# Backward-pass side jobs in another order, and one piece of a zero fill copied inside HBM

## The chip, the cores and the metric

The kernel runs on one core of one Trainium2 chip. Its time is device time in microseconds (us), the median of three runs. A profile of one execution stands beside it: its span is the time from the first to the last instruction that the profiler saw. Besides the compute engines TensorE (PE), VectorE (DVE), ScalarE (ACT) and GpSimd (POOL), the core has 16 DMA engines that carry every transfer. Two engines issue transfers here: SP puts them on the hardware queue (q1 in the profile), POOL on the software queue (q0). Both queues run on the same 16 DMA engines.

## The reference

One token passes a layer of grouped-query attention over the last W = 4096 rows of a key and a value cache, and a gated linear feed-forward layer; wanted are the output and the gradients of eight inputs, everything in bfloat16:

```python
k = jnp.repeat(k_cache[:, :, Sk - W:, :], rep, axis=1)      # Sk = 32768, W = 4096, 8 kv heads, Dh = 256
v = jnp.repeat(v_cache[:, :, Sk - W:, :], rep, axis=1)
scores = jnp.einsum("bhqd,bhkd->bhqk", q, k) * (Dh ** -0.5)
o = jnp.einsum("bhqk,bhkd->bhqd", _softmax(scores), v)
h = x + (o reshaped) @ wo
h2 = h + ((hn @ w_gate) * (hn @ w_up)) @ w_down             # hn = layernorm(h)
_out, _vjp = jax.vjp(_f, A_x, A_k_cache, A_v_cache, A_wq, A_wo, B_w_gate, B_w_up, B_w_down)
return (h2, *grads)
```

The gradients of the two caches have the caches' full shape (8 heads x 32768 rows x 256), and only the last 4096 rows of each head can be other than zero. So 2 x 8 regions of 28672 rows are zeros that the kernel has to write: 234.88 MB. The window parts of these gradients are 33.6 MB, the windows that are read some 34 MB, and the gradients of the weights (outer products of two vectors) are small beside them.

## The kernel before

**The fill.** A tile `zeros` of 128 x 8192 bfloat16 (16 KB in a partition) is cleared by DVE (line 54). SP then issues 16 transfers, one for each head `g` and each cache gradient (`out_2` for the keys, `out_3` for the values; lines 55 to 58). Each writes one region of 14,336 KB: seven pieces of 16 KB for each partition, all read from `zeros`. SP does nothing else. The hardware queue holds a bit more than two of them, and SP stands in the issue of the next until there is room.

**Everything else** goes through POOL's queue (`IO`): the small vectors `x_bf` and `go_bf` (lines 88, 90), the weights, the K and V windows of 2 MB each (line 75), and all other outputs.

**Forward** (up to line 399): for each of eight heads, scores, softmax and moments, then the feed-forward layer; eight slots of `S` hold windows and weights in turn.

**Backward** (lines 400 to 445): the gradients of the feed-forward layer's gates, then of `h`, then `doT`, and at line 453 `dq`. Behind it stand eight stages, one for each kv head `g` (lines 546 to 595). A stage transposes the V window on PE (line 554), forms `dp` (line 559), builds rows for an outer product (line 572), and in 16 steps of line 588 makes the gradients of 4096 key rows and 4096 value rows in PSUM, which ACT and DVE copy in turn into two of four staging slots of `S` (helper `evac`, lines 210 and 212). Two transfers of 2 MB store them (line 593). A stage may use a staging slot only when the stores of two stages before have landed.

**Side jobs.** After its stores each stage runs jobs from the table `side` (lines 521 to 531): `outer` (lines 472 to 477) writes one part of a weight gradient: DVE scales rows into one of two staging buffers of `Mt` (line 476) and POOL stores it (line 477), so a third call waits until the first one's store has landed. `ffn_out` (lines 490 to 501) loads `w_down` again and makes the output `h2`. `dxn_part` (lines 507 to 511) loads a part of `wq` again into `Rt` (4 of 7 blocks, then 3), and DVE multiplies it with `dq` and sums (line 510); `dx_out` then finishes the gradient of `x`. The second part goes into the same place in `Rt` as the first and must wait for it; the first must wait for `ffn_out`, which keeps `w_down` there.

The program's order is the order of the text only roughly: a scheduler places the instructions of each engine, and each engine then runs its own list strictly in order. So an instruction of a side job that waits for a transfer holds up what stands behind it on its engine.

Of the kernel before, what the change touches and what calls it, by code (L numbers as in the profile page):

```python
# [7 lines left out]
bf16 = mybir.dt.bfloat16  # L8
# [5 lines left out]
D = 448  # L14
# [4 lines left out]
W = 4096  # L19
# [3 lines left out]
Sk = 32768  # L23
# [5 lines left out]
HQ = H * Dh // 2  # L29
HF = F // 2  # L30
ZW = 8192
NZ = (Sk - W) * Dh // (128 * ZW)
# [8 lines left out]
def kernel(  # L41
# [4 lines left out]
    FILL = nc.sync  # L46
    IO = nc.gpsimd

    const = ctx.enter_context(tc.tile_pool(name="const", bufs=1))
    small = ctx.enter_context(tc.tile_pool(name="small", bufs=2))  # L50
    ps = ctx.enter_context(tc.tile_pool(name="ps", bufs=1, space=bass.MemoryType.PSUM))

    zeros = const.tile([128, ZW], bf16)
    V_.memset(zeros[:], 0.0)
    for g in range(G):
        for o in (out_2, out_3):
            reg = o[0, g, 0:Sk - W, :].rearrange("s d -> (s d)").rearrange("(p n f) -> p n f", p=128, f=ZW)
            FILL.dma_start(out=reg, in_=zeros[:].unsqueeze(1).to_broadcast([128, NZ, ZW]))


    S = const.tile([128, NS, SLOT], bf16)
# [22 lines left out]
        return w.rearrange("a b -> (a b)").rearrange("(p x) -> p x", p=128)  # L84


    x_bf = const.tile([1, D], bf16, tag="rowa", name="x_bf")
    IO.dma_start(out=x_bf[:], in_=A_x.rearrange("a b d -> (a b) d"))
    go_bf = const.tile([1, D], bf16, tag="rowb", name="go_bf")
    IO.dma_start(out=go_bf[:], in_=grad_out.rearrange("a b d -> (a b) d"))  # L90
    wq_sb = S[:, 1:3, :].rearrange("p a b -> p (a b)")[:, 0:NI * HQ]
    IO.dma_start(out=wq_sb, in_=flat_rows(A_wq))
    load_K(0)
# [126 lines left out]
    rstd1, xh1, xf1, xx1 = layernorm(xX[:], "ln1")  # L220
# [121 lines left out]
    bc2 = [S[:, 7, NI * HF:NI * HF + F].rearrange("p (i c) -> p i c", i=2), Rt[:, NI * HF:NI * HF + F].rearrange("p (i c) -> p i c", i=2)]  # L342
# [43 lines left out]
    rstd2, xh2, xf2, xx2 = layernorm(hX[:], "ln2")  # L386
# [44 lines left out]
    dh_bc = const.tile([128, D], bf16)  # L431
# [30 lines left out]
    dq_bc = late[:, 0:2 * HQ].rearrange("p (i c) -> p i c", i=2)  # L462
# [41 lines left out]
    wq2 = Rt[:, 0:4 * HQ].rearrange("p (i c) -> p i c", c=HQ)  # L504
    wq_d = flat_rows(A_wq).rearrange("p (i c) -> p i c", i=NI)

    def dxn_part(i0, i1):
        IO.dma_start(out=wq2[:, 0:i1 - i0, :], in_=wq_d[:, i0:i1, :])
        for i in range(i0, i1):
            V_.tensor_tensor_reduce(out=wq2[:, i - i0, :], in0=wq2[:, i - i0, :], in1=dq_bc[:, i % 2, :], scale=1.0, scalar=0.0,  # L510
                                    op0=ALU.mult, op1=ALU.add, accum_out=Pq[:, i:i + 1])

    def dx_out():
# [4 lines left out]
        V_.tensor_copy(out=dx[:], in_=t[:])  # L518
        IO.dma_start(out=out_1.rearrange("a b d -> (a b) d"), in_=dx[:])

    side = {
        0: [lambda: outer(o6, 0, 4, lambda i: bc2[0][:, i % 2, :], xf2, HF), lambda: outer(o6, 4, 7, lambda i: bc2[0][:, i % 2, :], xf2, HF),
            lambda: outer(o7, 0, 4, lambda i: bc2[1][:, i % 2, :], xf2, HF), lambda: outer(o7, 4, 7, lambda i: bc2[1][:, i % 2, :], xf2, HF)],
        1: [ffn_out] + [lambda b=b: outer(o5, b, b + 8, lambda n: dh_bc[:], oT_f, D) for b in (0, 8)],
        2: [lambda b=b: outer(o5, b, b + 8, lambda n: dh_bc[:], oT_f, D) for b in (16, 24)],
        3: [lambda b=b: outer(o8, b, b + 7, lambda n: dh2_bc[:], hh, D) for b in (0, 7)],
        4: [lambda: dxn_part(0, 4)],
        5: [lambda: dxn_part(4, 7), dx_out],
        6: [lambda i=i: outer(o4, i, min(i + 2, 7), lambda n: dq_bc[:, n % 2, :], xf1, HQ) for i in (0, 2)],
        7: [lambda i=i: outer(o4, i, min(i + 2, 7), lambda n: dq_bc[:, n % 2, :], xf1, HQ) for i in (4, 6)],  # L530
    }


    STG = [5, 6, 7, 0]
# [91 lines left out]
```

## Time and profile before

| what | value |
|---|---|
| time, median of 3 runs | 818.56 us (818.16 to 818.86) |
| the profiled execution: its time, its span | 818.39 us, 816.6 us |
| busy: PE, DVE, ACT, POOL | 497.6, 376.8, 164.9, 41.7 us |
| moved by DMA | 338.66 MB, mean 415 GB/s |
| of it hardware queue (the fill) | 234.88 MB, 68.2% of the DMA engines' span |
| of it software queue | 103.00 MB, 30.2% |
| HBM read, written | 57.28 MB, 280.59 MB |

The shares of the two queues are the time that their packets took, as a part of 16 engines' span. A share of DMA near 1 in a stretch means that all 16 DMA engines moved packets all the time in it (packets that overlap slightly can bring it to 1.01). The compute engines are all far from full, so what one of them waits for matters only where a transfer starts late by it and a DMA engine stands idle for that.

### The profile page before, as it was taken

How to read it: one execution, taken by the hardware profiler on the slowest of the kernel's cores; microseconds unless marked ns; L12 is line 12 of the kernel's file. 1: busy time of each engine (PE TensorE's matmuls, PEld its weight loads, DVE VectorE, ACT ScalarE, POOL GpSimd, SP SyncE). 2: the span in 40 equal slices, each digit the busy share in tenths (PEclk: the TensorE clock that was granted, in tenths of full speed). 3: DMA queues.
4: the chain of work that ended last, by engine and by line, in shares of the span. 5: the costliest groups of instructions: out<-in, count | busy, mean ns of one | idle time of the engine just before them, and what ended most of it. 6: DMA issues, size and time to landing. Idle time of an engine off the chain costs nothing.

```text
span 816.6 us, 12117 instructions
## 1 busy us (share of the span) xinstructions
PE 497.6 (61%) x4947; PEld 300.9 (37%) x4991; DVE 376.8 (46%) x1149; ACT 164.9 (20%) x261; POOL 41.7 (5%) x77
## 2 busy tenths in 40 slices
PE   3558869999574946062993468799378940001770
PEld 3545646666343523031981332345124410001110
DVE  4127847667461643028732354565255440404550
ACT  0220201221101000000011233355244420000440
POOL 4000000000000001000000000010010000000000
PEclk9959888999695969565555556555555555555555
DMA  8999999999999999999999999999999999999985
GB/s 322 431 424 429 427 429 426 429 427 426 432 423 426 424 420 418 427 429 432 423 430 427 417 413 426 428 402 429 419 404 426 423 428 400 424 415 432 431 355 237
DMA packets 24632, 338.66 MB, mean 415 GB/s; under 512 B 1312, under 2 KB 1376, under 8 KB 4736
## 3 DMA queue, kind: packets, MB, share of 16 engines
q1 hardware_dynamic: 14592, 234.88, 68.2%
q0 software_dynamic: 9984, 103.00, 30.2%
q8 instruction: 39, 0.64, 0.3%
q14 instruction: 17, 0.14, 0.0%
HBM read 57.28 MB, written 280.59 MB: 414 GB/s over the span
## 4 chain that ended last, share of the span: by engine, by line
issue 50%; DMA 22%; PE 14%; another core or an unknown queue 4%; DVE 4%; POOL 2%; ACT 1%; POOLq 0%; DVEq 0%; ACTq 0%
DMA out_dram<-Mt 9%; DMA out_dram<-S 5%; DMA S<-in_A_wo_dram 4%; PE dq_ps L453 3%; PE d_ps L588 3%; PE tr L554 2%; DMA S<-in_A_v_cache_dram 2%; DMA S<-in_A_wq_dram 2%; PE MT L322 2%; DVE Rt L423 1%; DVE Rt L510 1%; POOL S L75 1%; PE dh_ps L159 1%; DVE S L212 1%
## 5 line engine op out<-in xcount | busy, mean ns | idle before, releaser
L322 PE MATMUL MT<-Rt,S 128*128 128x512 bf16 x468 | 146.7, 391 | 22.5 <-DMA S<-in_A_v_cache_dram 19.8
L588 PE MATMUL d_ps<-R,Mt 32*128 32x512 bf16 x256 | 121.1, 605 | 58.6 <-DVE S L212 57.9
L318 DVE TENSOR_SCALAR Rt<-S,pf 128x256 bf16<-128x256 bf16 x512 | 118.0, 282 | 31.6 <-PE acc L329 16.5
L212 DVE CAST S<-d_ps 128x512 bf16<-128x512 f32 x128 | 87.1, 689 | 63.4 <-ACT S L210 55.6
L210 ACT CAST S<-d_ps 128x512 bf16<-128x512 f32 x128 | 74.9, 586 | 127.7 <-PE d_ps L588 127.7
L266 PE MATMUL tr<-ident_bf,S 128*128 128x128 bf16 x512 | 51.5, 264 | 43.4 <-DMA S<-in_A_k_cache_dram 40.1
L325 PEld LDWEIGHTS <-S 128*128 128x128 bf16 x512 | 50.1, 99 | 62.9 <-issue 7.2
L554 PE MATMUL tr<-ident_bf,S 128*128 128x128 bf16 x512 | 67.6, 304 | 0.7 <-ACT Mt L210 0.7
L588 PEld LDWEIGHTS <-Mt 32*128 32x128 bf16 x256 | 22.8, 113 | 112.8 <-issue 110.8
L329 PE MATMUL acc<-ones_bf,Rt 128*128 128x1 bf16 x1024 | 62.0, 164 | 0.0
L554 PEld LDWEIGHTS <-S 128*128 128x128 bf16 x512 | 48.4, 136 | 24.4 <-issue 24.4
L266 PEld LDWEIGHTS <-S 128*128 128x128 bf16 x512 | 40.5, 120 | 41.9 <-DMA S<-in_A_k_cache_dram 40.6
L325 PE MATMUL acc<-pT_all,S 128*128 128x2 bf16 x512 | 49.3, 166 | 2.6 <-issue 0.9
L165 PE MATMUL t<-st,ones_f 128*128 128x2 f32 x4 | 1.2, 364 | 79.6 <-DVE st L196 79.6
L210 ACT COPY Rt<-tr 128x1024 bf16<-128x1024 bf16 x32 | 32.4, 1012 | 85.1 <-PE tr L266 84.6
L210 ACT COPY Mt<-tr 128x1024 bf16<-128x1024 bf16 x32 | 32.4, 1014 | 60.8 <-PE tr L554 34.3
L329 PEld LDWEIGHTS <-Rt 128*128 128x128 bf16 x1024 | 44.5, 96 | 0.0
L212 DVE COPY Rt<-tr 128x1024 bf16<-128x1024 bf16 x32 | 22.1, 689 | 47.5 <-PE tr L266 46.2
L322 PEld LDWEIGHTS <-S 128*128 128x128 bf16 x512 | 32.2, 97 | 22.3 <-DMA S<-in_A_v_cache_dram 20.0
L331 ACT COPY Mt<-MT 128x512 f32<-128x512 f32 x8 | 4.7, 586 | 165.1 <-remote 73.8
L510 DVE CUSTOM_DVE_ANT_0 Rt<-Rt,Mt 128x2048 bf16<-128x2048 bf16 x7 | 15.6, 2289 | 48.3 <-DMA Rt<-in_A_wq_dram 48.3
L212 DVE COPY Mt<-tr 128x1024 bf16<-128x1024 bf16 x32 | 22.0, 686 | 22.9 <-PE tr L554 15.5
(184 smaller groups left out, 463.5 us busy)
## 6 DMA issues: line engine op xcount, KB each, us to landing
out_dram<-zeros SPq DMA_DIRECT2D x16, 14336.0 KB, 155.7
out_dram<-S POOLq DMA_DIRECT2D x16, 2048.0 KB, 31.0
S<-in_A_v_cache_dram POOLq DMA_DIRECT2D x11, 2048.0 KB, 35.6
S<-in_A_k_cache_dram POOLq DMA_DIRECT2D x8, 2048.0 KB, 27.9
out_dram<-Mt POOLq DMA_DIRECT2D x6, 896.0 KB, 18.2
S<-in_A_wq_dram POOLq DMA_DIRECT2D x1, 3584.0 KB, 15.3
S<-in_A_wo_dram POOLq DMA_DIRECT2D x2, 1792.0 KB, 35.6
out_dram<-Mt POOLq DMA_DIRECT2D x3, 1024.0 KB, 32.5
```

The costliest lines, as they stand in the source:

```text
L75: IO.dma_start(out=dst, in_=cache[0, g, Sk - W:, :].rearrange("(p t) d -> p t d", t=T))
L210: S_.copy(out=out, in_=in_)
L212: V_.tensor_copy(out=out, in_=in_)
L266: P_.transpose(tr[:, i, dh, :], Xw[:, 4 * q + i, dh * 128:(dh + 1) * 128], ident_bf[:])
L318: V_.tensor_scalar(out=pk[:, i, h, :], in0=K[:, t, :], scalar1=pf[:, t, h:h + 1], scalar2=None, op0=ALU.mult)
L322: P_.matmul(MT[:, hf, :], lhsT=Vv[:, t, hf * 128:(hf + 1) * 128], rhs=pk[:, i, :, :].rearrange("p h d -> p (h d)"), start=(t == 0), stop=( ...
L325: P_.matmul(acc[:, 2 * hf:2 * hf + 2], lhsT=Vv[:, t, hf * 128:(hf + 1) * 128], rhs=pT_all[:, g, t, :], start=(t == 0 and hf == 0), stop=(t ...
L329: P_.matmul(acc[:, 4 + 2 * h + dk:5 + 2 * h + dk], lhsT=pk[:, i, h, dk * 128:(dk + 1) * 128], rhs=ones_bf[:, 0:1], start=False, stop=(t == ...
L453: P_.matmul(dq_ps[:, 2 * h + dk:2 * h + dk + 1], lhsT=Mt[:, h // 2, hf, c0:c0 + 128], rhs=doT_f[:, 2 * h + hf:2 * h + hf + 1], start=(hf = ...
L510: V_.tensor_tensor_reduce(out=wq2[:, i - i0, :], in0=wq2[:, i - i0, :], in1=dq_bc[:, i % 2, :], scale=1.0, scalar=0.0, op0=ALU.mult, op1=A ...
L554: P_.transpose(tr[:, i, dh, :], Vw[g][:, 4 * q + i, dh * 128:(dh + 1) * 128], ident_bf[:])
L588: P_.matmul(d_ps[:, i, :, :].rearrange("p w d -> p (w d)"), lhsT=rows[32 * k:32 * k + 32, a, :], rhs=R[32 * k:32 * k + 32, :], start=True, ...
```

## The change

Three things change.

1. **The small vectors.** `x_bf` and `go_bf` (0.9 KB each) are loaded by SP, ahead of the fill, and no longer by POOL ahead of `wq`.
2. **One fill in two parts.** For head 4 of `out_3`, the tenth of the 16 fills, five of the seven 16 KB pieces of each partition still come from `zeros`; the last two are copied as one piece of 32 KB from the region of `out_2` that the first fill has cleared. That is 128 x 32 KB = 4.2 MB, read from HBM and written to HBM.
3. **The side jobs.** `ffn_out`, the two parts of the gradient of `w_up` (`o7`) and the load of the first four blocks of `wq` now stand ahead of the stages. `dxn_part` loses its load, which becomes `dxn_load`; the sums over `wq` and `dx_out` move from stages 4 and 5 to stages 0 and 1. The other jobs move: `o5` from stages 1 and 2 to 2 and 3, `o8` from 3 to 4, `o4` from 6 and 7 to 5 and 6. The last stage has none.

```diff
+    x_bf = const.tile([1, D], bf16, tag="rowa", name="x_bf")
+    FILL.dma_start(out=x_bf[:], in_=A_x.rearrange("a b d -> (a b) d"))
+    go_bf = const.tile([1, D], bf16, tag="rowb", name="go_bf")
+    FILL.dma_start(out=go_bf[:], in_=grad_out.rearrange("a b d -> (a b) d"))
     zeros = const.tile([128, ZW], bf16)
     V_.memset(zeros[:], 0.0)
     for g in range(G):
         for o in (out_2, out_3):
             reg = o[0, g, 0:Sk - W, :].rearrange("s d -> (s d)").rearrange("(p n f) -> p n f", p=128, f=ZW)
-            FILL.dma_start(out=reg, in_=zeros[:].unsqueeze(1).to_broadcast([128, NZ, ZW]))
+            if g == 4 and o is out_3:
+                FILL.dma_start(out=reg[:, 0:NZ - 2, :], in_=zeros[:].unsqueeze(1).to_broadcast([128, NZ - 2, ZW]))
+                src = out_2[0, 0, 0:Sk - W, :].rearrange("s d -> (s d)").rearrange("(p n f) -> p n f", p=128, f=ZW)
+                FILL.dma_start(out=reg[:, NZ - 2:NZ, :].rearrange("p n f -> p (n f)"), in_=src[:, 0:2, :].rearrange("p n f -> p (n f)"))
+            else:
+                FILL.dma_start(out=reg, in_=zeros[:].unsqueeze(1).to_broadcast([128, NZ, ZW]))
...
-    x_bf = const.tile([1, D], bf16, tag="rowa", name="x_bf")
-    IO.dma_start(out=x_bf[:], in_=A_x.rearrange("a b d -> (a b) d"))
-    go_bf = const.tile([1, D], bf16, tag="rowb", name="go_bf")
-    IO.dma_start(out=go_bf[:], in_=grad_out.rearrange("a b d -> (a b) d"))
...
+    def dxn_load(i0, i1):
+        IO.dma_start(out=wq2[:, 0:i1 - i0, :], in_=wq_d[:, i0:i1, :])
+
     def dxn_part(i0, i1):
-        IO.dma_start(out=wq2[:, 0:i1 - i0, :], in_=wq_d[:, i0:i1, :])
...
     side = {
-        0: [lambda: outer(o6, 0, 4, ...), lambda: outer(o6, 4, 7, ...),
-            lambda: outer(o7, 0, 4, ...), lambda: outer(o7, 4, 7, ...)],
-        1: [ffn_out] + [lambda b=b: outer(o5, b, b + 8, ...) for b in (0, 8)],
-        2: [lambda b=b: outer(o5, b, b + 8, ...) for b in (16, 24)],
-        3: [lambda b=b: outer(o8, b, b + 7, ...) for b in (0, 7)],
-        4: [lambda: dxn_part(0, 4)],
-        5: [lambda: dxn_part(4, 7), dx_out],
-        6: [lambda i=i: outer(o4, i, min(i + 2, 7), ...) for i in (0, 2)],
-        7: [lambda i=i: outer(o4, i, min(i + 2, 7), ...) for i in (4, 6)],
+        0: [o67_job(0, 0, 4), o67_job(0, 4, 7), lambda: dxn_part(0, 4), lambda: dxn_load(4, 7)],
+        1: [lambda: dxn_part(4, 7), dx_out],
+        2: [o5_job(0), o5_job(8)],
+        3: [o5_job(16), o5_job(24)],
+        4: [lambda b=b: outer(o8, b, b + 7, lambda n: dh2_bc[:], hh, D) for b in (0, 7)],
+        5: [o4_job(0), o4_job(2)],
+        6: [o4_job(4), o4_job(6)],
+        7: [],
     }
+    ffn_out()
+    o67_job(1, 0, 4)()
+    o67_job(1, 4, 7)()
+    dxn_load(0, 4)
```

`o4_job`, `o5_job` and `o67_job` return the same `outer` calls as the lambdas before. The instructions of DVE and ACT stay the same in number (PE has one more), and so do the bytes that are written; 4.2 MB more are read from HBM and as many less from `zeros`.

More of the change, by code (lines that the diff above doesn't have):

```diff
@@ L519, in dx_out, with o4_job, o5_job, o67_job @@
         IO.dma_start(out=out_1.rearrange("a b d -> (a b) d"), in_=dx[:])
-    side = {
[L522 to L526, printed above, removed]
-        4: [lambda: dxn_part(0, 4)],
-        5: [lambda: dxn_part(4, 7), dx_out],
-        6: [lambda i=i: outer(o4, i, min(i + 2, 7), lambda n: dq_bc[:, n % 2, :], xf1, HQ) for i in (0, 2)],
-        7: [lambda i=i: outer(o4, i, min(i + 2, 7), lambda n: dq_bc[:, n % 2, :], xf1, HQ) for i in (4, 6)],
-    }
+    def o4_job(i):
+        return lambda: outer(o4, i, min(i + 2, 7), lambda n: dq_bc[:, n % 2, :], xf1, HQ)
+    def o5_job(b):
+        return lambda: outer(o5, b, b + 8, lambda n: dh_bc[:], oT_f, D)
+    def o67_job(w, i0, i1):
+        return lambda: outer((o6, o7)[w], i0, i1, lambda i: bc2[w][:, i % 2, :], xf2, HF)
+    side = {
+        0: [o67_job(0, 0, 4), o67_job(0, 4, 7), lambda: dxn_part(0, 4), lambda: dxn_load(4, 7)],
[6 more added lines that the diff above has]
+        7: [],
+    }
+    ffn_out()
+    o67_job(1, 0, 4)()
+    o67_job(1, 4, 7)()
+    dxn_load(0, 4)
     STG = [5, 6, 7, 0]
```

## The prediction

> **What bounds the kernel now.** I read the page first, for how full the DMA engines are.
>
> ```profile
> span 816.6 us, 12117 instructions
> ...
> DMA  8999999999999999999999999999999999999985
> GB/s 322 431 424 429 427 429 426 429 427 426 432 423 426 424 420 418 427 429 432 423 430 427 417 413 426 428 402 429 419 404 426 423 428 400 424 415 432 431 355 237
> ...
> q1 hardware_dynamic: 14592, 234.88, 68.2%
> q0 software_dynamic: 9984, 103.00, 30.2%
> ```
>
> The DMA row is full from the second slice to the 38th. The 338.66 MB bound the kernel; no compute engine does (PE 61%). So a wait on an engine costs time only if a DMA engine stands idle by it. Next I asked for windows of time (columns: stretch, its length, busy time of PE, PE's weight loads, DVE, ACT, POOL, then clock, DMA share, GB/s).
>
> ```profile
> 0.00:20.00 20.00, 7.46 (x32) 7.12 (x32) 9.36 (x47) 1.54 (x2) 8.57 (x23) 1.00 0.82 320
> 100.00:280.00 180.00, 142.25 (x2027) 96.41 (x2055) 104.19 (x428) 26.29 (x45) 3.17 (x6) 0.86 1.01 427
> 480.00:560.00 80.00, 70.90 (x513) 31.97 (x511) 43.23 (x85) 35.17 (x53) 6.44 (x10) 0.54 1.01 417
> 680.00:720.00 40.00, 0.00 (x0) 0.00 (x0) 8.94 (x8) 0.00 (x0) 1.58 (x3) 0.50 1.01 407
> 790.00:794.00 4.00, 3.41 (x8) 0.80 (x8) 2.08 (x3) 1.70 (x4) 0.00 (x0) 0.50 0.58 246
> 794.00:798.00 4.00, 2.17 (x5) 0.34 (x3) 2.61 (x4) 1.86 (x4) 0.27 (x1) 0.50 0.35 147
> 798.00:804.00 6.00, 0.00 (x0) 0.00 (x0) 0.16 (x1) 0.00 (x0) 0.79 (x2) 0.50 0.93 390
> ...
> 808.00:812.00 4.00, 0.00 (x0) 0.00 (x0) 0.00 (x0) 0.00 (x0) 0.00 (x0) 0.50 0.30 127
> 812.00:817.00 5.00, 0.00 (x0) 0.00 (x0) 0.00 (x0) 0.00 (x0) 0.00 (x0) 0.50 0.03 13
> ```
>
> At 427 GB/s the bytes would take 793.1 us; the span has 23.5 more. They lie in three places. First 20 us: 20 x (427 - 320)/427 = 5.0. Slow but full stretches of the backward pass (417 at 480 to 560, 407 at 680 to 720, and smaller ones): 1.9 + 1.9 + about 2.6. From 790 to the end: 27 us that move 6.2 MB, worth 14.4, so 12.6 lost.
>
> The last of these looks like the prize. POOL's timeline says why the engines idle there, the list of waits where it began:
>
> ```profile
> 778.05 0.55 POOL L593 DMA_DIRECT2D out_dram<-S  x1 [23.30 <-ACT S L210]
> 797.73 0.53 POOL L593 DMA_DIRECT2D out_dram<-S  x1 [18.42 <-ACT S L210]
> ```
>
> ```profile
> ACT R L579 <- PE R_ps L577: 84.6, 4, 81.2
> DVE Rt L510 <- DMA Rt<-in_A_wq_dram: 48.3, 2, 24.9
> ```
>
> DVE, in order, waited 24.9 and 23.4 us for the two parts of `wq`; stages 6 and 7 stood behind it, and ACT was without work for 81.2 us (to 756). So the last stores were issued at 797.7, when the fill was done on most DMA engines.
>
> On most, not on all. The 4-byte completion packets of the last fill (packet records of the trace, one on each engine) come at 777.6 on the first engine, 784.9 on the tenth, 805.1 on the last; those of the tenth fill at 463.4 on the first, 473.1 on the fifteenth, 482.7 on the last. One DMA engine is thus behind through half of the run. Fills are always queued until 777.6, so no engine idles before; the last one has packets until it finishes the final store at 814.2, while the fifteen others wait for those stores. **The end is set by one DMA engine that never rests from about 4 us on.** An earlier store cannot shorten it; only less work on that engine, or an earlier first packet, can.
>
> **The change, part by part**
>
> **Small vectors.** Before, POOL spends 0.62 and 0.50 us on them ahead of `wq`:
>
> ```profile
> 1.31 0.62 POOL L88 DMA_DIRECT2D x_bf<-in_A_x_dram  x1 [0.85 <-POOLq L610]
> 1.93 0.50 POOL L90 DMA_DIRECT2D go_bf<-in_grad_out_dram  x1
> 2.42 0.55 POOL L92 DMA_DIRECT2D S<-in_A_wq_dram  x1
> ```
>
> `wq` moves up by 1.1 us, and the engines, which have nothing until 3 to 4 us, start by as much earlier: **-1.1 us** on every engine. On SP two issues of some 0.6 us come ahead of the first fill, which waits until 5.1 for the clearing of `zeros` (1.67 to 5.14): they cost nothing. Without that cover it would be 1.3 us of a fill, which `wq` and the windows would hide in turn, since they fill the engines until 9 us.
>
> **Side jobs.** The DVE sums (7 of 2.29 us), the two `wq` loads (2048 and 1536 KB), `h2`, `o7`, `o5`, `o8` and `o4` change place on POOL's queue but not in number: as DMA work they sum to 0. On POOL's list the first `wq` load now stands after three stores of `o7` and `o6` and before the first window stores, so it waits for some 2 MB and not for the 4 MB of a stage; the second stands behind a V load. DVE's wait for them moves into stage 0; half of its evacuations stand behind it. Before, stores follow each other by about 34 us (503.6, 537, 570, 604.7, 641.6, 675.3), then by 102. With stage 0 some 5 to 20 us later (below the 24.9 that the old wait took) and a cadence of 34, the last pair goes out at 503.6 + 5 to 20 + 7 x 34 = 747 to 762, a good 30 us before 797.7. After that the fill alone keeps all engines busy. This removes idle time of fifteen engines; for the last engine it is **0**.
>
> What may change for it is the slow stretches. At 680 to 720 stores, a `wq` load and `o4` met the fill and 1.9 us were lost. The meeting dissolves, but the loads and stores still run beside the fill elsewhere. Bounds: -1.9 (it vanishes) and +1.9 (another stretch like it forms). I take half of the gain, **-0.9**, since the tail becomes fill alone, which runs at 427 and more.
>
> **The copy.** 4.19 MB at 427 GB/s are 9.8 us of every DMA engine, as before. The trace has no transfer from HBM to HBM. Nearest row: at 100 to 280 windows are read from HBM while fills are written to it, at 427 GB/s, as fast as anything here. Lower end: 0 (a piece of 28 KB in the trace is no faster per byte than one of 16 KB). Upper end: a DMA engine that spends its time once for the read and once for the write, +9.8. I take **0**. SP's wait ahead of it (a semaphore that it shares with an earlier fill) and the cleared source are long past: the first fill landed before 70 us, this one is issued past 390.
>
> A rule speaks against it. By the Trainium skill, HBM Reference, section Specifications (TRN2), the HBM of two cores gives about 716 GB/s in all; the trace, at 427, shows no such limit. An estimate from that page: a copy, which reads and writes there, gets at most half, 358 GB/s, 11.7 us for 9.8, and the sum would be -0.1. The page DMA: Bandwidth & Descriptors, section Latency and other measured facts, gives 214 GB/s per direction at best for copies between HBM tensors, an estimate of 19.6 us, and the sum would be +7.8.
>
> **Sum:** -1.1 + 0 - 0.9 + 0 = -2.0 us: 818.39 to 816.4 for the profiled execution, and 816.6 for the median, which stands 0.17 above it.
>
> **Rivals**
>
> *The copy is dear (slower).* If the engine pays twice, -2.0 + 9.8 = +7.8: 826.4. For: no row shows such a copy, and all engines would read and write HBM at once. Against: the engine behind reaches its copy some 10 us after the others, so it may have HBM more to itself. It decides from a surcharge of 20% on (2.0 of 9.8); from 37% on the kernel is slower by 0.2%. A middling surcharge of 50% gives 821.5.
>
> *The tail evens out (faster).* If the engine that is behind owes its delay to the meeting of stores and fill, all engines end together: of the 12.6 us in the tail 2.4 are the fixed end after the last landing, so up to -10 - 1.1, about 807.5; half of it 812. Against: it was behind already at 300 us, before any store.
>
> *The waits only move.* DVE stalls in stage 0 and then at each staging buffer, and the last stores go out later than 797.7: each us past about 797 costs one. At 802, some 820. It takes 35 us more than I estimate.
>
> *No difference.* The copy's surcharge or a new slow stretch eats the gain of the start: 817.5 to 819.
>
> **How the numbers follow.** My forecast has 0.42 (own range 814.5 to 817.5), the dear copy 0.24, no difference 0.16, the even tail 0.10, moved waits 0.08. The range 811.5 to 824 leaves out the far half of the even tail (0.05) and the dearest copies and waits (0.11). A measurement tells about 0.2% (1.6 us) from no change: faster is 0.36 of my forecast's and the even tail's 0.10, 0.46; the same 0.24 (no difference, the rest of mine, a cheap surcharge); slower 0.30.
>
> **What would show it.** POOL's `wq` issue at 1.3 and a higher first slice; ACT's wait of 81 us gone and the last stores before 770; a DMA row full until some 800, then a tail in which only few engines move fill packets; the last landing belongs to the fill. The copy's 32 KB packets should take twice a 16 KB packet of the fill: some 1.2 us, against 2.4 if I am wrong. I am also wrong if the stretch around the copy falls well below 427 GB/s, or if POOL's last issue is past 797.

## The result, and the profile after

The changed kernel takes 816.69 us (median of 11 runs, 816.38 to 817.56), the kernel before 818.56 us in the same comparison. By these medians it is faster by 1.9 us, 0.23%; the forecast was 816.6. The ratio of the comparison, 0.9963 with a 95% interval of 0.9947 to 0.9978, says 0.37%, because it does not go by the medians: of the 11 executions of the kernel before three took 821 to 823 us, of the changed kernel none over 817.6.

The profiled execution took 816.38 us. First its page, with the lines that answer to those shown of before:

```profile
span 814.6 us, 12156 instructions
...
DMA  8999999999999999999999999999999999999993
GB/s 344 428 425 426 430 427 430 426 429 423 433 424 426 427 416 421 425 428 432 427 430 426 402 427 428 431 424 418 429 409 428 424 419 418 421 426 424 425 430 146
...
q1 hardware_dynamic: 14484, 234.88, 68.2%
q0 software_dynamic: 9920, 103.00, 30.2%
```

The first slice moves 344 GB/s where it moved 322. The 39th is full (430; before 355), and only the last one falls off. The fill and the software queue carry the same bytes as before. The windows show both ends closer (columns: stretch, its length, busy time of PE, PE's weight loads, DVE, ACT, POOL, the granted clock, DMA share, GB/s):

```profile
0.00:20.00 20.00, 7.46 (x32) 7.12 (x32) 9.45 (x47) 1.54 (x2) 7.23 (x21) 1.00 0.87 341
...
780.00:800.00 20.00, 0.00 (x0) 0.00 (x0) 0.00 (x0) 0.00 (x0) 0.00 (x0) 0.50 0.96 410
800.00:808.00 8.00, 0.00 (x0) 0.00 (x0) 0.00 (x0) 0.00 (x0) 0.00 (x0) 0.50 0.23 96
808.00:814.60 6.60, 0.00 (x0) 0.00 (x0) 0.00 (x0) 0.00 (x0) 0.00 (x0) 0.50 0.05 20
```

From 780 us on no compute engine works any more. The engines move fill to about 800, then a few of them, and after 808 a share of 0.05, which is about one engine of sixteen. POOL's timeline gives the first load and the last stores (start, duration, engine, line, operation, and in brackets the idle time before it and what ended that):

```profile
1.29 0.67 POOL L97 DMA_DIRECT2D S<-in_A_wq_dram  x1 [0.84 <-POOLq L629]
...
765.61 0.53 POOL L612 DMA_DIRECT2D out_dram<-S  x1 [16.41 <-ACT S L215]
766.34 0.53 POOL L612 DMA_DIRECT2D out_dram<-S  x1 [0.19 <-issue]
```

`wq` is asked for 1.13 us earlier (1.29 for 2.42), and the last pair of stores 32 us earlier (765.6 for 797.7). The list of waits has ACT's 81 us behind the sums over `wq` no more; its largest group is now spread over 115 waits, none above 20 us:

```profile
ACT S L215 <- PE d_ps L607: 165.3, 115, 19.6
```

The packet records say what sets the end. The completion packets of the last fill come at 791.4 to 806.3 us on fifteen engines and at 813.0 on the sixteenth. The software queue's last landing, the end in the profile before, is over at 803.2.

So the difference between the two profiled executions, 2.0 us, has two halves. The last landing of all moved from 814.2 to 813.0 (1.1 us). And the time from there to the end of the span shrank from 2.44 to 1.57 us (0.9 us). The second half was in no term of the prediction.

### The profile page after: what moved, and what is told of

The parts are those of the page before. It is cut to its first block, busy times and chain, and to the rows that moved or that the text cites. A ratio compares the mean times of both kernels' runs of the same rounds, so it can differ in the third digit from the quotient of the medians.

```text
span 814.6 us, 12156 instructions
## 1 busy us (share of the span) xinstructions
PE 509.2 (63%) x4991; PEld 304.8 (37%) x4991; DVE 374.4 (46%) x1149; ACT 165.0 (20%) x261; POOL 40.4 (5%) x75
## 4 chain that ended last, share of the span: by engine, by line
issue 59%; DMA 17%; PE 11%; DVE 4%; POOL 3%; ACT 1%; POOLq 0%; DVEq 0%
DMA S<-in_A_wo_dram 4%; DMA out_dram<-Mt 4%; DMA Rt<-in_A_wq_dram 4%; PE dq_ps L458 3%; DMA S<-in_A_k_cache_dram 3%; DMA S<-in_A_v_cache_dram 2%; PE MT L327 2%; POOL out_dram L482 1%; POOL S L84 1%; DVE Rt L428 1%; POOL out_dram L612 1%; PE dh_ps L164 1%; PE ao L388 1%; PE d_ps L607 1%; PE tr L573 1%
## 5 line engine op out<-in xcount | busy, mean ns | idle before, releaser
L607 PE MATMUL d_ps<-R,Mt 32*128 32x512 bf16 x256 | 124.4, 612 | 88.0 <-DVE S L217 87.3
L327 PE MATMUL MT<-Rt,S 128*128 128x512 bf16 x512 | 157.5, 392 | 21.7 <-DMA S<-in_A_v_cache_dram 20.3
L271 PE MATMUL tr<-ident_bf,S 128*128 128x128 bf16 x512 | 54.7, 274 | 43.5 <-DMA S<-in_A_k_cache_dram 40.2
L330 PEld LDWEIGHTS <-S 128*128 128x128 bf16 x512 | 50.0, 99 | 63.1 <-issue 7.2
L573 PE MATMUL tr<-ident_bf,S 128*128 128x128 bf16 x512 | 68.8, 304 | 3.5 <-ACT Mt L215 3.5
L573 PEld LDWEIGHTS <-S 128*128 128x128 bf16 x512 | 48.5, 135 | 28.0 <-issue 27.8
L271 PEld LDWEIGHTS <-S 128*128 128x128 bf16 x512 | 42.9, 124 | 42.0 <-DMA S<-in_A_k_cache_dram 40.7
L327 PEld LDWEIGHTS <-S 128*128 128x128 bf16 x512 | 32.2, 97 | 22.4 <-DMA S<-in_A_v_cache_dram 20.9
L578 PEld LDWEIGHTS <-Mt 128*128 128x128 bf16 x512 | 20.0, 108 | 41.8 <-DVE Mt L217 18.8
L578 PE MATMUL dp<-doT,Mt 128*128 128x2 bf16 x512 | 22.6, 168 | 17.3 <-DVE Mt L217 15.6
L217 DVE COPY Mt<-tr 128x1024 bf16<-128x1024 bf16 x32 | 22.0, 686 | 16.4 <-PE tr L573 11.3
```

Of the source, the lines that this page charges most:

```text
L217: V_.tensor_copy(out=out, in_=in_)
L271: P_.transpose(tr[:, i, dh, :], Xw[:, 4 * q + i, dh * 128:(dh + 1) * 128], ident_bf[:])
L327: P_.matmul(MT[:, hf, :], lhsT=Vv[:, t, hf * 128:(hf + 1) * 128], rhs=pk[:, i, :, :].rearrange("p h d -> p (h d)"), start=(t == 0), stop=( ...
L330: P_.matmul(acc[:, 2 * hf:2 * hf + 2], lhsT=Vv[:, t, hf * 128:(hf + 1) * 128], rhs=pT_all[:, g, t, :], start=(t == 0 and hf == 0), stop=(t ...
L573: P_.transpose(tr[:, i, dh, :], Vw[g][:, 4 * q + i, dh * 128:(dh + 1) * 128], ident_bf[:])
L578: P_.matmul(dp[:, 4 * q + i, :], lhsT=xt[:, i, dh, :], rhs=doT[:, 4 * g + dh:4 * g + dh + 3:2], start=(dh == 0), stop=(dh == 1))
```

## The experiments

Two theories stood at the beginning. The prediction's: one DMA engine ends last because it has more to do than the others, so only an earlier start or less work for it helps, and a copy of 4.2 MB costs it nothing. Its rival: the chain of the stores sets the end, the new order of the side jobs brings the gain, and the copy takes back a part of it.

### Each part alone

Without the copy, the rest of the change kept (the tenth fill is written from `zeros` like the others):

```diff
-            if g == 4 and o is out_3:
-                FILL.dma_start(out=reg[:, 0:NZ - 2, :], in_=zeros[:].unsqueeze(1).to_broadcast([128, NZ - 2, ZW]))
-                ...
-            else:
-                FILL.dma_start(out=reg, in_=zeros[:]...)
+            FILL.dma_start(out=reg, in_=zeros[:]...)
```

> The changed kernel without the copy: all 16 fills come from zeros. My theory (the DMA engine that is behind sets the end; the copy costs that engine about what the fill does): 816.0 to 816.9, the lower end if the 32 KB packets' mean of 1330 ns against 2 x 619 ns (8 packets an engine, 0.7 us) counts in full. Rival, the copy brings the gain: 818 or more. Rival, the copy is dear and hides a larger gain: below 815.

The kernel before, with the two small vectors on SP alone:

```diff
+    FILL.dma_start(out=x_bf[:], in_=...)     # ahead of the fill, on SP
+    FILL.dma_start(out=go_bf[:], in_=...)
...
-    IO.dma_start(out=x_bf[:], in_=...)       # on POOL, ahead of wq
-    IO.dma_start(out=go_bf[:], in_=...)
```

> The kernel before, with the two small vectors on SP alone. My theory: every DMA engine starts 1.1 us earlier and the one that never rests ends 1.1 us earlier: 817.4 (ratio 0.9987). Rival, idle time of the tail is what counts: last stores still go out near 797, so 818.5.

The kernel before, with the new order of the side jobs alone:

```diff
+        0: [o67_job(0, 0, 4), o67_job(0, 4, 7), lambda: dxn_part(0, 4), lambda: dxn_load(4, 7)],
+        1: [lambda: dxn_part(4, 7), dx_out],
...
+    ffn_out()
+    o67_job(1, 0, 4)()
+    o67_job(1, 4, 7)()
+    dxn_load(0, 4)
```

> The kernel before, with the side jobs in the new order alone (vectors on POOL, no copy). My theory: the engine that is behind has the same work, so 818.5 less what the end after the last landing gets shorter (2.4 us in the profile before, 1.5 after): about 817.6, and the last landing still at 813.5 to 814.5. Rival, the tail's idle time: 12.6 us of it go, time 808 to 815.

Measured on one chip, but for the last row:

| kernel | median, us (lowest to highest) | ratio to before, 95% interval | last pair of stores issued | last landing: fill, software queue |
|---|---|---|---|---|
| before (landings: first profile) | 819.17 (818.07 to 824.34) | | 797.7, 798.5 | 805.1, 814.2 |
| vectors alone | 818.63 (817.2 to 822.02) | 0.9983 (0.9962 to 1.0003) | 801.3, 802.0 | 802.8, 814.4 |
| order alone | 817.34 (816.99 to 817.48) | 0.9965 (0.995 to 0.9981) | 763.4, 764.2 | 814.4, 801.0 |
| both, no copy | 816.47 (816.24 to 816.91) | 0.9957 (0.994 to 0.9974) | 763.1, 763.8 | 813.5, 799.9 |
| the whole change (first comparison) | 816.69 (816.38 to 817.56) | 0.9963 (0.9947 to 0.9978) | 765.6, 766.3 | 813.0, 803.2 |

The copy cannot be told from nothing: 0.2 us at the most by the medians, and the intervals overlap widely. The two other edits don't add up. The vectors alone gain nothing that is sure: 818.6 is the number of the rival (818.5), not of the theory (817.4). Only the best of their 12 executions, 817.2 and 817.3, lie about a microsecond below the best of the kernel before, 818.1. In the profiled execution (818.47 us) the stores came out even later than before (POOL's timeline):

```profile
801.27 0.53 POOL L593 DMA_DIRECT2D out_dram<-S  x1 [18.42 <-ACT S L210]
801.99 0.53 POOL L593 DMA_DIRECT2D out_dram<-S  x1 [0.20 <-issue]
```

In the packet records its last store lands at 812.3 on most engines and at 814.4 on the last; in the kernel before, 808.8 and 814.2. So the stores' chain, 3.5 us later, has come up to the late engine, which is not done 1.1 us earlier, as the theory has it. That it had to wait for its last packets is likely but not shown, for the records name no engine. The two limits lay close together from the start, 5.4 us apart in the kernel before. The start's gain is safe only when the order of the side jobs has moved the stores out of the way. Why the stores came out later here was not followed.

With the order alone the stores leave 34 us earlier:

```profile
763.44 0.53 POOL L607 DMA_DIRECT2D out_dram<-S  x1 [16.41 <-ACT S L210]
764.17 0.53 POOL L607 DMA_DIRECT2D out_dram<-S  x1 [0.20 <-issue]
```

And the last landing does not move at all: 814.4 for 814.2. Thirty-four microseconds on the chain of stores are worth nothing at the landing, as the prediction's theory has it. But the profiled execution is still 0.9 us shorter (817.45 for 818.39), because only 1.3 us follow the last landing and not 2.4. The medians differ by more, 1.8 us, for with the new order the times spread over 0.5 us, and over 6 before. The stores may have set the end in the long executions, but none of them was profiled, so this is not shown.

### What a copy costs when every engine copies

The prediction had bounds of 0 and +9.8 for the copy and no row for it. Here 24 copies of 4.2 MB, 100.7 MB in all, take the place of six of the seven pieces in the last eight fills, in pieces of 32 KB:

```diff
-            if g == 4 and o is out_3:
-                FILL.dma_start(out=reg[:, 0:NZ - 2, :], in_=zeros[:]...)
+            if g >= 4:
                 src = out_2[0, 0, 0:Sk - W, :]...
+                FILL.dma_start(out=reg[:, 6:7, :], in_=zeros[:].unsqueeze(1).to_broadcast([128, 1, ZW]))
+                for k in (0, 2, 4):
+                    FILL.dma_start(out=reg[:, k:k + 2, :]..., in_=src[:, k:k + 2, :]...)
```

> The changed kernel with 24 copies of 4.2 MB instead of one (six of seven pieces of the last eight fills, 100.7 MB, 236 us of every DMA engine at 427 GB/s). Copy at the price of a fill: 817. With the surcharge that the 32 KB packets show in the changed kernel (1330 for 1238 ns, 7%): 833. Half of HBM's rate as the page's 716 GB/s allow (358 GB/s): 862. Read and write paid apart: 1050.

Measured: 864.05 us, ratio 1.0536 (1.0506 to 1.0565). The windows show the copy's rate, where copies were most of the traffic, and in a later stretch:

```profile
400.00:420.00 20.00, 20.00 (x97) 20.00 (x98) 12.29 (x46) 1.01 (x1) 0.00 (x0) 0.50 1.00 349
520.00:540.00 20.00, 0.00 (x0) 0.00 (x0) 0.00 (x0) 0.00 (x0) 0.00 (x0) 0.50 0.99 398
```

All engines are busy (1.00) and move 349 GB/s, where the kernel without a copy moves 427 in the same stretch: a surcharge of 22%. But that is not what made the kernel as slow as this. Its fills and copies were done at 806.2, while POOL's last stores went out at 850:

```profile
849.76 0.53 POOL L613 DMA_DIRECT2D out_dram<-S  x1 [16.40 <-ACT S L216]
850.49 0.53 POOL L613 DMA_DIRECT2D out_dram<-S  x1 [0.19 <-issue]
```

The software queue had been starved. A new guess was that the two queues take turns by packets, so that a queue with packets of 32 KB takes more than its share from one with smaller ones. The test: the same bytes, copied in pieces of 16 KB.

```diff
-                for k in (0, 2, 4):
-                    FILL.dma_start(out=reg[:, k:k + 2, :]..., in_=src[:, k:k + 2, :]...)
+                for k in range(6):
+                    FILL.dma_start(out=reg[:, k, :], in_=src[:, k, :])
```

> The kernel with 24 copies again, but 48 copies in pieces of 16 KB. In that kernel the fill was done at 806 and the last stores went out at 850: the software queue had got less than its half. If that is because a turn of the hardware queue moves 32 KB against 16 KB (my theory now), it gets its half back, the stores go out earlier, and what is left is the price of copying (347 GB/s where nothing else ran, 400 in the mix): 830 to 845. If it is the copying itself that holds up the software queue: 864 again.

Measured: 841.87 us, ratio 1.0272 (1.0242 to 1.0302). The software queue was done at 786.6, the fills and copies at 837.9; the end has changed hands again. The rate of the copies is about the same as with 32 KB at 400 to 420, and the later stretch, where the software queue moves half of the bytes, is full speed. At 790 to 815, with the software queue done, nearly all the traffic is copies:

```profile
400.00:420.00 20.00, 20.00 (x95) 20.00 (x96) 13.36 (x50) 1.01 (x1) 0.00 (x0) 0.50 1.01 357
520.00:540.00 20.00, 20.00 (x149) 10.11 (x146) 11.09 (x26) 8.21 (x12) 0.63 (x2) 0.50 1.01 429
790.00:815.00 25.00, 0.00 (x0) 0.00 (x0) 0.00 (x0) 0.00 (x0) 0.00 (x0) 0.50 1.00 334
```

So the surcharge of a copy reaches 28% (427 against 334). The 22 us between the two kernels come from the size of the pieces (and with it the number of transfers, 48 for 24). The packet records show the turns themselves: at 600 to 700 us the hardware queue and the software queue moved 1,100 and 1,103 packets with pieces of 32 KB, and 1,758 and 1,763 with pieces of 16 KB. And the copies as such cost 25.4 us for 100.7 MB (841.87 less the 816.47 without a copy); by that rate one copy of 4.2 MB costs 1.1 us. The whole change pays less, and its own windows say where (first the changed kernel, then the one without the copy):

```profile
440.00:450.00 10.00, 6.63 (x60) 3.94 (x60) 6.06 (x12) 2.18 (x3) 1.97 (x4) 0.50 1.01 418
450.00:460.00 10.00, 2.03 (x30) 1.50 (x27) 0.63 (x3) 1.01 (x1) 0.16 (x1) 0.50 1.06 408
460.00:470.00 10.00, 5.45 (x70) 4.72 (x71) 3.10 (x10) 3.04 (x3) 0.00 (x0) 0.50 0.94 396
```

```profile
440.00:450.00 10.00, 8.18 (x87) 5.45 (x86) 4.14 (x8) 3.20 (x4) 2.14 (x4) 0.50 1.01 423
450.00:460.00 10.00, 4.24 (x55) 3.64 (x54) 3.30 (x10) 1.89 (x2) 0.00 (x0) 0.50 1.00 425
460.00:470.00 10.00, 7.05 (x71) 4.68 (x72) 5.44 (x12) 3.86 (x6) 1.44 (x2) 0.50 1.01 396
```

At 450 to 460, when most engines copy at once, the rate is 408 and not 425, and single packets of 32 KB take up to 2,375 ns. But those engines have time. The one that is behind comes to its copy about 13 us after the others, at 470 to 482 us. Its own packets take 1,231 to 1,312 ns, where two packets of 16 KB of the fill take 1,222: some 0.3 us for its eight pieces.

### Which engine is last, and why

A store of k short rows has k packets, taken here to lie on the first k of the sixteen engines, one on each. Two such stores behind each of the later fills, with one row less each time, show at which k the late engine drops out:

```diff
+            if g >= 2:
+                for _ in range(2):
+                    if nprobe > 0:
+                        FILL.dma_start(out=cut[0:nprobe, ...], in_=zeros[0:nprobe, 0:32])
+                    nprobe -= 1
```

> The changed kernel with 15 tiny stores of 64 bytes a row on SP's queue between the later fills, over 15 rows, then 14, and so on down to one; a part of the last 1 KB of 128 rows of one zero region (what the tiny stores do not reach) stays unwritten. If a store of k rows goes to the k lowest DMA engines, the engine that is behind shows its number: its packet comes some 10 us after the others in every store that has it and is absent from the others. My theory: one and the same engine is late in all of them, so late packets are there for all k above some number. Rival (engines take turns in being behind): late packets without such an order. Time 816 to 819.

Measured: 817.36 us (one run). The 64-byte packets in the packet records:

```
rows of the two stores   the late packets (us)     all the others (us)
13, 12                   318.3, 319.2              302.9 to 310
11, 10                   363.6, 363.6
 9,  8                   401.1, 401.4
 7,  6                   438.9, 438.9              the next latest 432.3, 432.7
 5,  4                   485.8, one only           the next latest 479.1, 479.7
 3,  2                   none                      518.1 to 518.8
```

With five rows the late packet is there, with four it isn't. If the stores fill the engines in order, as these packets fit, the late engine is the fifth, the same one all the time, and the fourth is the second latest. So it is not chance, and not the stores' work that collects somewhere. That engine has a load of its own. The page of the profile offers a candidate: queue 8, `instruction`, 39 packets of 16 KB, 0.64 MB. For TensorE's 9,982 instructions that is 64 bytes each, one packet for 256 of them. (The expectations below put them at 9,410, too few.) The test was to take a fifth of TensorE's instructions away:

```diff
-                for h in range(2):
+                for h in range(2 if t == T - 1 else 0):
                     for dk in range(2):
                         P_.matmul(acc[:, 4 + 2 * h + dk:...], lhsT=pk[...], rhs=ones_bf[:, 0:1], ...)
```

> The changed kernel without 31 of 32 of PE's matmuls that sum the weighted keys (1984 of PE's 9411 instructions; the gradient of wq comes out wrong by that). PE's instructions are fetched by 39 transfers of 16 KB on queue q8, on these same DMA engines. If one engine carries all of them and is behind for that reason, some 8 fetches of 0.6 us go: the last landing comes 4.7 us earlier, time 812. If the fetches are spread over the engines, or the delay has another cause: 816.3 to 816.7.

Measured: 812.72 us, ratio 0.9914 (0.9894 to 0.9934), 4.0 us below the changed kernel. But that run also left out a part of TensorE's work, and its gradient of `wq` with it, so a rival remained: the chain of stores got shorter, and that was the gain. The counter-test adds instructions that nobody waits for:

```diff
+    for b in range(200):                       # ahead of the product with wo
+        P_.matmul(ao[0:1, 0:1], lhsT=one, rhs=one, start=True, stop=True)
...
+                P_.matmul(d_ps[0:1, i, 0, 0:1], lhsT=one, rhs=one, start=True, stop=True)   # one for each step of a stage
...
+    for b in range(200):                       # after the last stage
+        P_.matmul(d_ps[0:1, 0, 0, 0:1], lhsT=one, rhs=one, start=True, stop=True)
```

> The changed kernel without the copy and with 656 matmuls of one element more, nobody's input (200 before the product with wo, where TensorE waits 27 us for a load, one before each matmul of the gradient rows, 200 after the last): 1,312 instructions of TensorE with their weight loads, 84 KB, some 5 fetches of 16 KB more. If the fetches lie on the DMA engine that ends last, each costs 0.47 us (the run with 8 fetches less, 3.75 us) to 0.6 us (a fetch's own duration): 818.8 to 819.6 in place of 816.5. The rival: fetches are spread or that run gained by its shorter TensorE work: then 816 to 817 here, since the stores still come out some 10 us before the last engine ends.

Measured: 819.16 us, ratio 0.9990 (0.9976 to 1.0004), 2.7 us above the kernel without the copy on which it is built (measured in another comparison). From the pages, first 1,984 instructions less (built on the changed kernel, copy included), then the kernel without the copy, then 1,312 more:

```profile
span 810.8 us, 9967 instructions
...
q8 instruction: 31, 0.51, 0.2%
```

```profile
span 815.1 us, 12155 instructions
...
q8 instruction: 39, 0.64, 0.3%
```

```profile
span 817.1 us, 13417 instructions
...
q8 instruction: 44, 0.72, 0.3%
```

With 31, 39 and 44 fetches the last fill lands at 809.3, 813.5 and 815.4 on the late engine. On the middle one of the sixteen it lands at 799.3, 800.4 and 800.7. With the instructions added, the last stores went out at 768.0 and 768.7 (763.1 and 763.8 without them), and the software queue was done at 803.3, 12 us before the end: the chain of stores had nothing to do with it. So it goes both ways, and mainly on the one engine: it carries the instruction fetches of TensorE, and each costs the kernel 0.4 to 0.5 us (4.0/8 and 2.7/5 by the medians; 1.9/5 by the last landing). The late engine's lag behind the middle one, 10.0, 13.1 and 14.7 us, is 0.32 to 0.34 us for each fetch in all three: as far as three points tell, the fetches account for about the whole of it. The expectation called 0.6 us a fetch's own duration; the records of queue 8 say 0.95 us, so about half of it or more seems to pass beside other packets.

### Attempts to make use of it

If a fetch costs half a microsecond, fewer instructions for the same result should gain. In the forward stage the sums over V and over the weighted K were taken with six narrow matmuls for each tile of 128 keys. As rows they need two of 256 columns:

```diff
-                for hf in range(2):
-                    P_.matmul(acc[:, 2 * hf:2 * hf + 2], lhsT=Vv[:, t, ...], rhs=pT_all[:, g, t, :], ...)
-                for h in range(2):
-                    for dk in range(2):
-                        P_.matmul(acc[:, 4 + 2 * h + dk:...], lhsT=pk[...], rhs=ones_bf[:, 0:1], ...)
+                for w, X in ((0, Vv), (1, K)):
+                    P_.matmul(acc[:, w, :], lhsT=pT_all[:, g, t, :], rhs=X[:, t, :], ...)
...
+        (four transposes for each head bring the rows back into columns)
```

> The changed kernel without the copy, with the two sums of the backward pass taken as rows: two matmuls of 256 columns per tile of keys in place of six narrow ones, and four transposes per head more; some 2,040 of TensorE's 9,410 instructions fall away and nothing is left out. The theory: TensorE's instruction fetches lie on the one DMA engine that ends last, so by the run that left out 1,984 instructions (816.5 to 812.7) this one ends at 812 to 813.5, with some 31 fetches in place of 39. The rival: that run gained by the work that it left out (fewer waits behind TensorE), and then this one, which has the same sums to take, stays at 816 to 817.

Measured: 827.74 us, ratio 1.0096 (1.0071 to 1.0121). The fetches fell to 31, but the expectation was wrong by 15 us. The windows say why (first the rows, then the kernel without the copy):

```profile
100.00:250.00 150.00, 142.49 (x1099) 55.62 (x1111) 83.98 (x340) 22.78 (x41) 2.12 (x4) 0.96 1.01 428
750.00:800.00 50.00, 38.88 (x163) 11.90 (x163) 33.89 (x55) 22.23 (x38) 4.30 (x8) 0.50 0.72 299
```

```profile
100.00:250.00 150.00, 120.50 (x1720) 80.98 (x1716) 88.44 (x367) 22.25 (x41) 3.17 (x6) 0.86 1.01 427
750.00:800.00 50.00, 9.19 (x20) 1.90 (x18) 7.61 (x11) 6.37 (x11) 1.07 (x2) 0.50 1.00 423
```

TensorE, with fewer instructions, is busy for 142 of 150 us instead of 120 and bounds the forward stage. Everything behind it comes later, and POOL's last stores with it:

```profile
812.92 0.53 POOL L609 DMA_DIRECT2D out_dram<-S  x1 [16.40 <-ACT S L210]
813.65 0.53 POOL L609 DMA_DIRECT2D out_dram<-S  x1 [0.19 <-issue]
```

The fill is done at 764.4 on the late engine, then the DMA engines wait for the stores (0.72 busy in the last stretch). The run shows nothing on the fetches. It shows where the cover of the present order ends. The last stores go out 50 us later than without the rows (813.7 for 763.8) and cost 11.3 us, so the chain of stores had some 38 us to spare; the 13 us between the landings (799.9 against 813.5) say too little, for those stores shared the engines with the fill.

The other way is to give the late engine less of the fill. With the rows kept, each engine's last 16 KB row of three fills is left out, and 15 of the 16 rows go to three engines, taken to be the lowest:

```diff
+            if g in (1, 2, 3) and o is out_3:
+                FILL.dma_start(out=reg[:, 0:NZ - 1, :], in_=zeros[:]...)
+                FILL.dma_start(out=last[0:112, :], in_=zeros[0:112, :])
+                FILL.dma_start(out=last[112:127, :].rearrange("(e n) f -> e n f", e=3), in_=zeros[0:24:8, :]...)
+                FILL.dma_start(out=last[127, :]..., in_=...)        # split over all 16
```

> The run before, and in three of the fills each of the sixteen DMA engines gets one row of 16 KB less and the rows left over go to the three lowest engines, five each in each fill: three packets of 0.6 us, 1.8 us, less on the engine that ends last, and some 7 us more on each of three engines. If that engine sets the end and the three lowest have that much room (their last packets of the fill landed before the last engine's by 7 us or more), it ends at 810.5 to 811.5. If the three lowest become the last, or another engine was about as late as the last one, it ends at or above the run before it.

Measured: 857.32 us, ratio 1.0424 (1.0367 to 1.0481): 30 us slower again. Packets of 16 KB took over 1 us in and behind each of the three changed fills (41 of them at 280 to 290 us alone, where a normal one takes 611 ns). So the next run took TensorE's work as it was, and wrote the relieved fills in contiguous pieces, 55 rows on each engine, from one SBUF partition for each engine:

```diff
+                FILL.dma_start(out=flat[0:880, :].rearrange("(e n) f -> e n f", e=16),
+                               in_=zeros[0:128:8, :].unsqueeze(1).to_broadcast([16, 55, ZW]))
+                FILL.dma_start(out=flat[880:895, :].rearrange("(e n) f -> e n f", e=3), in_=zeros[0:24:8, :]...)
+                FILL.dma_start(out=flat[895, :]..., in_=...)        # split over all 16
```

> The changed kernel without the copy, TensorE's work as it was, and in three of the fills every DMA engine writes 55 rows of 16 KB in place of 56; fifteen of the rows left over go to the three lowest engines, five each, and the last is split over all sixteen. Each engine reads its own SBUF partition throughout, and each piece of the region is contiguous. That takes 1.8 us (three packets) from the engine that ends last and puts about 7 us on each of three others, which were done with their fill 5 to 13 us before it. If one engine sets the end, 816.5 goes to 814.5 to 815; if the three are the last now or the second latest engine is in the way, to 816 or more; if the short stores to three engines slow all the others as in the run before, to over 818.

Measured: 974.42 us, ratio 1.1766 (1.1705 to 1.1826). It got far worse. The last run kept all of this but the places written: each engine's piece begins 896 KB from the next one's and not 880. (That the ordinary fill has this spacing is the expectation's reading; the records name no places.)

```diff
-                FILL.dma_start(out=flat[0:880, :].rearrange("(e n) f -> e n f", e=16), ...)
+                FILL.dma_start(out=rows[:, 0:55, :], ...)      # rows: the region as 16 x 56 x 16 KB
```

> The last relief again with one thing changed: each engine's 55 rows begin where its 56 rows begin in the ordinary fill, 896 KB from the next engine's, and not 880 KB; the row left over lies at the end of each piece. Sources, row counts and the three engines that take the rest stay. If the spacing of the sixteen places written made 16 KB packets last 1,120 to 1,280 ns in place of 611 ns in the run before (265 GB/s in its slow stretches), they last 611 ns here, and the relief shows: 814.5 to 815 if one engine alone sets the end, 816 to 818 if the uneven rows cost as much as they give. If the source (one SBUF partition for each engine through all 55 rows) or the short stores to three engines made them slow, this one is slow too: 900 and above by the source, 820 to 860 by the short stores.

Measured: 976.01 us (958.61 to 991.57); no interval is given for it. Its windows, before the first relieved fill and in it:

```profile
100.00:160.00 60.00, 47.77 (x690) 33.93 (x699) 33.77 (x139) 10.56 (x18) 1.06 (x2) 0.86 1.00 427
180.00:240.00 60.00, 38.10 (x506) 25.46 (x512) 26.00 (x107) 7.31 (x11) 0.53 (x1) 0.72 1.00 266
```

The DMA share is 1.00 in both, and the second moves 266 GB/s: packets of the fill that took 611 ns take 1,136 ns on the mean at 200 to 240 us. The step from 880 to 896 KB thus changes nothing. Nor are the short stores to three engines the cause: the slow packets begin at 172 us, when the engines get done with the third fill and begin the relieved one, and the short stores stand behind its 55 rows. Of the expectation's causes the source is left: the 16 KB rows come from every eighth partition of `zeros` and no longer from all 128. By the Trainium skill, DMA: Bandwidth & Descriptors, section The descriptor swizzle, partitions 0 to 3 and 32 to 35 lie on one SBUF port, and so on in groups of four, and in a transfer over 128 partitions each engine writes a port of its own. Every eighth partition would then lie on only eight of the sixteen ports, two engines on each. That fits packets of nearly twice the time, but a fill from sixteen partitions on sixteen ports, which would test it, was not run, and the order in which each engine writes its rows may differ from the ordinary fill's too. So the cause stays open, and the relief itself untested.

No version here beats the changed kernel with a complete result: 816.47 without the copy is the same within the measurement.

## Why the prediction was right, and where not

**The bound: right.** One engine never rests and sets the end. The order alone brought the stores forward by 34 us and the last landing by nothing. Fetches on that engine alone moved the end by 0.4 to 0.5 us each, down and up. The prediction did not know why this engine is behind; it is TensorE's instruction fetches, with about 0.33 us of lag for each.

**Small vectors, -1.1: right in size, but not on its own.** `wq` came 1.13 us earlier and the last landing 1.14 us earlier. Alone, the edit gave nothing that can be told (0.9983, interval up to 1.0003), most likely because the stores were then as late a limit; that was not tested. On top of the order it gave 0.9 us (817.34 to 816.47). The prediction added the edits as if they were independent; the cover under this term was the other edit, and the text did not name it.

**Side jobs, 0: right at the landing, wrong at the end.** Last stores before 770: right (766.3). The estimate of 747 to 762 was missed by 4 us: the first pair went out at 523.3, just within "5 to 20 us later", but the cadence was 34.6 us and not 34. The term is not 0 but -0.9 in the profiles, for the end after the last landing is shorter when that landing is the fill's: the prediction took the 2.4 us as "the fixed end". By the medians it is even -1.8 (819.17 to 817.34), since the order also ended the spread of the times, which no term had.

**Slow stretches, -0.9: the step that failed.** The stretches did get faster. The changed kernel moves 426 GB/s where it was 417, and 422 where it was 407:

```profile
480.00:560.00 80.00, 50.39 (x323) 22.87 (x321) 47.20 (x78) 25.37 (x40) 5.22 (x9) 0.50 1.01 426
680.00:720.00 40.00, 21.34 (x125) 7.98 (x125) 19.12 (x35) 11.50 (x19) 2.17 (x4) 0.50 1.01 422
```

But the last landing moved by 1.14 us, which the start explains alone, and with the order alone it did not move at all. The rates are of all sixteen engines together, and the prediction took a gain in them for a gain of the engine that ends last, against its own rule that only less work on that engine or an earlier first packet helps. The sum came out by chance: the end's 0.9, which was in no term, had the size of this one.

**The copy, 0 between 0 and +9.8: right.** The medians give 0.2 us, the late engine's own packets 0.3. The copy's 32 KB packets took 1,213 ns in the median, "some 1.2 us" as foreseen. But the reason given, a rate of 427 GB/s for reads and writes side by side, does not carry over to a copy: with all engines copying it was 334 to 357. The lesser point "the engine behind reaches its copy some 10 us after the others" did the work. By the Trainium skill, HBM Reference, section Specifications (TRN2), the estimate was 358 GB/s: the runs come close to it from below (349 and 357 where copies were most of the traffic, 334 where they were nearly all). The 214 GB/s per direction of the page DMA: Bandwidth & Descriptors, section Latency and other measured facts, is not a limit here: the 334 are above it by far.

**The rivals.** The dear copy "decides from a surcharge of 20% on": with all engines copying the surcharge is 20 to 28%, so this rival was nearer than its price of 826 made it look; it fell because one engine decides, and that one, with its copy behind the others', paid little. The even tail fell: with the stores out of the way fifteen engines are still done 7 to 22 us before the last. The moved waits fell at 766 us, 31 before the point where they cost; the run with the rows showed what lies behind that point (last stores at 813, time 828). The point itself lies later than the 797 of the prediction: in that run and in the one with 32 KB copies the end came 14.3 us after the last issue (813.7 to 827.9, 850.5 to 864.8), which puts it at about 802 for a time of 816.5. No difference fell, narrowly: its 817.5 is 0.8 us away.

## What to carry to other kernels

When all DMA engines look full, ask when each of them is done, not when the queue is: the last one of sixteen sets the end, and a gain of 34 us on a chain that ends before it moved the last landing by nothing. Look in the list of queues for traffic that lies on one engine alone, such as the instruction fetches; there a thousand instructions were worth 2 us. And before two edits are added up, ask which limit each one moves, and how far the next limit is behind.

## What the runs showed of the hardware that was not expected

- TensorE's instructions are fetched in packets of 16 KB, one for 256 instructions, 39 for this kernel. Their load lies on one of the sixteen DMA engines: each fetch made it lag by some 0.33 us and the kernel longer by 0.4 to 0.5.
- Two queues that both had work took turns by packets (1,100 and 1,103 of them in 100 us, whatever their size): 100.7 MB on one of them in packets of 32 KB starved the other, whose last stores went out at 850 us; in packets of 16 KB the other was done at 787.
- Copies from HBM to HBM on all engines moved 334 to 357 GB/s, the fill from SBUF 427 at 100 to 280 us of the same kernels.
- From the last landing to the end of the span it took 2.1 to 2.4 us in the five kernels where the software queue landed last, and 1.3 to 1.7 us in the nine where the hardware queue did.
- A fill read from 16 partitions, every eighth one, ran at 266 GB/s with all engines busy; from all 128 at 427.
